# A fused long-convolution and cosine feed-forward kernel: shorter transforms of batches 2 to 7, 29 instead of 31 main chunks, and a last part that begins 940 tokens sooner

## The chip, the core and the metric

The kernel runs on one core of a Trainium2 chip. The engines are PE (the matmuls; its weight loads are shown apart as PEld), DVE (vector), ACT (scalar), POOL (GpSimd) and SP (which issues most of the DMAs). Each engine works through its own instructions in a fixed order and waits on semaphores where it needs another engine's result. The metric is the device time of one execution in microseconds, lower is better; the number given is the median of several executions.

## What is computed

```python
def _attn_ref(x, filt_r, filt_i):            # x: 8 batches, 3008 tokens, 256 columns
    X = np.fft.rfft(x, axis=1)
    F = (filt_r + 1j * filt_i)[None, :, :]
    return np.fft.irfft(X * F, n=x.shape[1], axis=1)
...
def _moe_ref(x, w_in, w_out):                # the 24064 tokens as rows
    h = x @ w_in                             # 256 -> 2048
    g = h * np.cos(h)
    return g @ w_out                         # 2048 -> 256
```

All is float32. The kernel gets that accuracy from matmuls in a rounded format by splitting a value in a high and a low part and adding three products (high by high, low by high, high by low).

## The kernel before

**Transform.** 3008 is 47 times 64, so each batch's FFT is done in stages with small matrices on PE, and between the stages the data goes through DRAM. Of batches 1 to 7: `stage1` (32 pieces a batch: ACT and POOL split the loaded input, POOL at L358; PE multiplies at L363; DVE copies at L365; SP writes), then `stage23` (12 pieces a batch). A piece of `stage23` is loaded, POOL adds two halves (`zf`, L389), ACT rounds (`zh`, L393), POOL takes the low part (`zl`, L394), PE multiplies by the matrix `m2` (three matmuls, L286, L287, L288; the third needs `zl`) into one of two PSUM banks named `ps`, DVE multiplies by the filter (L404 four times, L405, L406; after L406 the bank is free), ACT and POOL split again (`yh` L409, `yl` L410), PE multiplies by `m3` (the same three lines, into the next `ps` bank), and ACT copies out (L419). `stage4` (units of 235 tokens: PE L555, ACT and DVE L576 to L590, POOL `y1` L591) makes the feed-forward part's input.

**Feed-forward, main part.** Tokens are taken in chunks (`SIZES`), each in 8 steps. A step is `hidden` (12 matmuls at L699, as wide as the chunk, into `hp`), the gate (ACT L709, DVE L710, ACT L713, DVE L714, ACT `gh` L719, POOL `gl` L720) and, two steps later, `project` (12 matmuls at L734). So a chunk takes 192 matmuls of its width.

**Feed-forward, last part.** The tokens from the end of the main chunks on are computed by a scheme of block products with 7 products in place of 8. A chunk there is four quads; a quad is 42 matmuls at L780, half as wide as the chunk (248 or 250 columns), and 24 at L864 of the chunk's width. The function `_wide` cuts the tokens into nearly equal chunks of at most 504. This part cannot begin before batch 7 is transformed, because its first operations combine tokens of different places (the flag is that all of batch 7's `z2` are written); eight DMAs (`load_sums`) bring prepared weight sums.

**What sets the order.** From the third chunk on PE's order is written out by hand: the program walks through the steps of the feed-forward part, and at each quarter step asks a list `due` which transform pieces are due. Time in that list is counted in slots: 64 slots are 470 tokens of a chunk, so a chunk of 510 has 69.4 slots. A piece that PE takes part in keeps at least 3 slots from the one before, except that a batch's `m3` of one piece and `m2` of a later one may stand together. Each batch is spread evenly between a start and an end:

```python
        start = FIRST if b == 1 else end + BETWEEN
        end = slot(NJ * TJ) - BEFORE + LATER if b == 1 else start + LENGTH
...
        step = (end - start - GAP12) / (ones + 2 * n23)
...
            t = start + step * (i - SOON + 1 if b == 1 else 2 * i + 1)
            plan(stage1(b, i), t - AHEAD1, [t, t + step][: b], split=t - SPLIT1 if b > 1 else None)
...
            t = start + step * (ones + 2 * i + 2) + GAP12
            g = stage23(b, i)
            plan(g, t - AHEAD2, [], lambda b=b: len(wrote1.get(b, ())) == 2 * n1, t - SPLIT2)
            due.extend([at, kind, g, lambda: True] for at, kind in ((t, SECOND), (t + 4 * step, THIRD)))
```

So `GAP12` is the pause between the two stages, in which the first stage's results reach DRAM and come back. The second stage's first instructions are emitted behind the gate that was emitted last: `zf` on POOL is tied behind that gate's `gl`, the cast on ACT behind that gate's cast. The order on ACT, DVE, POOL and SP is otherwise a scheduler's.

Of the kernel before, what the change touches and what calls it, by code (L numbers as in the profile page):

```python
# [29 lines left out]
SLOTS = 8  # L30
LAG = 2
APART = 3
FIRST, LENGTH, BETWEEN = 80, 260, 24
BEFORE, LATER = 140, 28
GAP12 = 28
AHEAD1, AHEAD2, AHEAD4 = 34, 36, 24
SPLIT1, SPLIT2 = 18, 20
HALF, WIDE = 252, 512
SIZES = [470] * 4 + [464] + [510] * 26
FROM4, APART4, LATE4, CLOSE4 = 12, 20, 2, 14  # L40
SUMS, EACH_SUM, KEEP = 64, 12, 9
LOAD_SUMS, EACH_LOAD = 2030, 8
AHEAD_UNIT, APART_TIED = 130, 4
AHEAD_BLOCK = (52, 48, 43, 38, 33, 28)
SOON = 4
# [132 lines left out]
def fft_filter_then_cos_glu(ctx: ExitStack, tc: tile.TileContext, ins, outT):  # L178
# [41 lines left out]
    def load_full(*names):  # L220
        for name in names:
            rows, cols = ins[name].shape
            shared = {"f1": "m1", "f1x": "m1", "f2": "m2", "f3": "m3", "f30": "m30"}.get(name)
            mats[name] = const.tile([P, 2 * cols if shared and rows == P else cols], F32, name=name, tag=shared or name)[:rows, :cols]
            nc.sync.dma_start(mats[name], ins[name])
# [8 lines left out]
    begins = [0]  # L234
    for size in SIZES:
        begins.append(begins[-1] + size)
# [293 lines left out]
    def stage4(u):  # L530
# [40 lines left out]
        else:  # L571
            parts = [(k, max(t0, begins[k]), min(t0 + size, begins[k + 1])) for k in range(len(SIZES)) if max(t0, begins[k]) < min(t0 + size, begins[k + 1])]
            flat = fft.tile([P, 512], F32, name="y4", bufs=1)[:, : NDT * size].rearrange("p (t n) -> p t n", t=NDT)
# [115 lines left out]
    def hidden(c, s):  # L689
        nt = SIZES[c]  # L690
        yh, yl = ys[c]
        assert filled[c] == nt, (c, filled)
        hp = ps_h.tile([P, 2, 512], F32, name="hp")
        for u in range(2):
            fs = slice(u * P, (u + 1) * P)
            for t in range(NDT):
                for n, (w, y) in enumerate(((0, yh), (0, yl), (1, yh))):
                    with tc.issue_after(last_h[0]) if c == s == 0 else nullcontext():
                        mm = nc.tensor.matmul(hp[:, u, :nt], w_in[s][w][:, t, fs], y[:, t, :nt],  # L699
                                              start=(t == 0 and n == 0), stop=(t == NDT - 1 and n == 2))  # L700
                if u == 0 or t == 0:
                    yield
        last_h[:] = [mm.ins]
        with tc.high_priority() if c == 0 else nullcontext():
            gs[c, s] = gate(hp[:, :, :nt], nt, nc.vector if c == 0 else nc.gpsimd)
# [18 lines left out]
    def project(c, s):  # L724
        nt = SIZES[c]
        if s == 0:
            accs[c] = [ps_o.tile([P, 512], F32, name=f"acc{e}") for e in range(2)]
        gh, gl = gs.pop((c, s))
        for e in range(2):
            acc = accs[c][e][:, :nt]  # L730
            es = slice(e * P, (e + 1) * P)
            for u in range(2):
                for n, (w, g) in enumerate(((0, gh), (1, gh), (0, gl))):
                    nc.tensor.matmul(acc, w_out[s][w][:, u, es], g[:, u],  # L734
                                     start=(s == 0 and u == 0 and n == 0),
                                     stop=(s == NFT // 2 - 1 and u == 1 and n == 2))
                if e == 0 or u == 0:
                    yield
        if s == NFT // 2 - 1:
            t0 = begins[c]  # L740
            for e in range(2):
                if stages:
                    o = fft.tile([P, 512], F32, name="o", tag="ld", bufs=5)[:, :nt]
                else:
                    o = opool.tile([P, 510], F32, name="o")[:, :nt]
                nc.scalar.activation(o, accs[c][e][:, :nt], AF.Copy, scale=TWO_PI)
                nc.scalar.dma_start(outT[e * P : (e + 1) * P, t0 : t0 + nt], o)
            del accs[c], ys[c]
# [234 lines left out]
    with tc.issue_after(last_x[0]):  # L983
        load_full("m40", "m41")
    steps = [(c, s) for c in range(len(SIZES)) for s in range(NS)]

# [33 lines left out]
    for b in range(1, B):  # L1020
        start = FIRST if b == 1 else end + BETWEEN
        end = slot(NJ * TJ) - BEFORE + LATER if b == 1 else start + LENGTH
        ones = n1 - SOON if b == 1 else 2 * n1
        step = (end - start - GAP12) / (ones + 2 * n23)
        for i in range(SOON if b == 1 else 0, n1):
            t = start + step * (i - SOON + 1 if b == 1 else 2 * i + 1)
            plan(stage1(b, i), t - AHEAD1, [t, t + step][: b], split=t - SPLIT1 if b > 1 else None)
        for i in range(n23):
# [4 lines that stand above are left out]
    for u in range(2, len(units)):  # L1033
# [10 lines left out]
        else:  # L1044
            k = max(k for k in range(len(SIZES)) if begins[k] <= t0)
            place = sum(begins[k] <= a < t0 for _, _, a in units)
# [157 lines left out]
```

## Time and profile before

| | |
|---|---|
| time, median of 3 executions | 2404.26 us (2403.96 to 2405.15) |
| the profiled execution's own time | 2405.0 us |
| its span | 2403.2 us |
| TensorE clock over the span, as a share | 0.997 |

Busy time is what an engine spends in instructions, and a bracket behind an instruction of a listing in order of time is the idle time just before it with what ended it. A listing gives the start in us, the busy time of the group, the engine, the line, the operation, the tiles and the shapes; the ends of matmuls are modelled, so prices of matmuls are taken from start to start.

### The profile page before, as it was taken

How to read it: one execution, taken by the hardware profiler on the slowest of the kernel's cores; microseconds unless marked ns; L12 is line 12 of the kernel's file. 1: busy time of each engine (PE TensorE's matmuls, PEld its weight loads, DVE VectorE, ACT ScalarE, POOL GpSimd, SP SyncE). 2: the span in 40 equal slices, each digit the busy share in tenths (PEclk: the TensorE clock that was granted, in tenths of full speed). 3: DMA queues.
4: the chain of work that ended last, by engine and by line, in shares of the span. 5: the costliest groups of instructions: out<-in, count | busy, mean ns of one | idle time of the engine just before them, and what ended most of it. 6: DMA issues, size and time to landing. Idle time of an engine off the chain costs nothing.

```text
span 2403.2 us, 35048 instructions
## 1 busy us (share of the span) xinstructions
PE 2367.4 (99%) x12127; PEld 1999.8 (83%) x12127; DVE 1641.4 (68%) x2328; ACT 1658.2 (69%) x2469; POOL 1820.3 (76%) x1465
## 2 busy tenths in 40 slices
PE   6999999999999999999999999999999999999999
PEld 2788888888888888878887888888999999999998
DVE  5846756766686677658666765855777777777776
ACT  4866676767677666767676776766767777676776
POOL 2777677978797787869787887956777777777775
PEclk9999999999999999999999999999999999999999
DMA  8745355545554554545445444540000000000000
GB/s 296 250 145 157 121 150 148 177 141 141 156 186 129 144 186 142 145 139 183 133 139 183 153 135 127 186 127 27 25 18 30 22 27 25 22 26 26 23 13 18
DMA packets 187433, 277.53 MB, mean 115 GB/s; under 512 B 19344, under 2 KB 102480, under 8 KB 187256
## 3 DMA queue, kind: packets, MB, share of 16 engines
q1 hardware_dynamic: 155448, 223.11, 31.0%
q10 hardware_dynamic: 31808, 52.18, 6.0%
q8 instruction: 97, 1.59, 0.3%
q14 instruction: 80, 0.66, 0.1%
HBM read 177.16 MB, written 98.06 MB: 115 GB/s over the span
## 4 chain that ended last, share of the span: by engine, by line
PE 89%; POOL 2%; DVE 2%; issue 1%; ACT 1%; DMA 0%; SPq 0%; ACTq 0%; POOLq 0%; DVEq 0%
PE acc L734 25%; PE hp L699 25%; PE acc L864 15%; PE x L780 8%; PE w L780 4%; PE ps L555 3%; PE ps L780 2%; PE ps L363 2%; PE ps L288 2%; PE ps L286 1%; PE ps L287 1%; POOL gl L720 1%; POOL zl L394 0%; POOL zf L389 0%; DVE g L710 0%
## 5 line engine op out<-in xcount | busy, mean ns | idle before, releaser
L720 POOL TENSOR_TENSOR gl<-g,gh 128x1020 fp32r<-128x1020 f32 (+2 forms) x240 | 570.8, 2378 | 236.5 <-ACT gh L719 129.4
L699 PE MATMUL hp<-y,w_in 128*128 128x510 f32 (+2 forms) x2976 | 737.7, 390 | 4.3 <-DVE g L714 3.6
L699 PEld LDWEIGHTS hp<-y,w_in 128*128 128x128 f32 x2976 | 560.7, 189 | 124.1 <-issue 5.3
L734 PE MATMUL acc<-gh,w_out 128*128 128x510 f32 (+2 forms) x1984 | 613.4, 391 | 0.0
L710 DVE TENSOR_TENSOR g<-g,hp 128x1020 f32<-128x1020 int32 (+2 forms) x248 | 297.9, 1201 | 203.8 <-ACT g L709 202.3
L734 PEld LDWEIGHTS acc<-gh,w_out 128*128 128x128 f32 x1984 | 367.9, 188 | 75.3 <-issue 2.0
L714 DVE TENSOR_TENSOR g<-g,hp 128x1020 f32<-128x1020 f32 (+2 forms) x248 | 297.7, 1201 | 133.0 <-ACT g L713 131.4
L734 PE MATMUL acc<-gl,w_out 128*128 128x510 f32 (+2 forms) x992 | 384.4, 389 | 0.7 <-POOL gl L720 0.5
L713 ACT ACTIVATE g<-g,half_pi 128x1020 f32<-128x1020 f32 (+2 forms) x248 | 282.5, 1139 | 147.6 <-DVE g L710 143.8
L719 ACT CAST gh<-g 128x1020 fp32r<-128x1020 f32 (+2 forms) x248 | 256.9, 1036 | 136.5 <-DVE g L714 135.5
L709 ACT ACTIVATE g<-hp 128x1020 int32<-128x1020 f32 (+2 forms) x248 | 250.2, 1009 | 141.4 <-PE hp L699 118.5
L358 POOL TENSOR_TENSOR xh<-xf,xh 48x512 fp32r<-48x512 f32 x192 | 244.4, 1292 | 0.0
L762 ACT ACTIVATE qg<-qg,half_pi 128x496 f32<-128x496 f32 (+1 forms) x272 | 187.4, 711 | 70.4 <-DVE qg L761 70.2
L734 PEld LDWEIGHTS acc<-gl,w_out 128*128 128x128 f32 x992 | 186.7, 188 | 41.3 <-POOL gl L720 2.1
L365 DVE COPY z1t<-ps 96x512 f32<-96x512 f32 x192 | 131.6, 685 | 114.1 <-PE ps L363 110.9
L404 DVE SCALAR_TENSOR_TENSOR sw<-ps,sg,f 64x256 f32<-64x256 f32 x336 | 162.4, 483 | 56.7 <-PE ps L288 51.7
L864 PE MATMUL acc<-hg,w_out 128*128 128x496 f32 (+1 forms) x548 | 183.8, 390 | 0.0
L864 PE MATMUL acc<-hgh,w_out 128*128 128x496 f32 (+1 forms) x544 | 182.9, 390 | 0.6 <-POOL hgh L842 0.6
L864 PE MATMUL acc<-hgl,w_out 128*128 128x496 f32 (+1 forms) x540 | 181.3, 390 | 0.0
L410 POOL TENSOR_TENSOR yl<-ya,yh 128x512 fp32r<-128x512 f32 x84 | 109.2, 1301 | 37.5 <-ACT yh L409 29.0
L786 ACT COPY sum<-x 128x496 f32<-128x496 f32 (+1 forms) x136 | 78.4, 577 | 63.7 <-PE x L780 63.4
L394 POOL TENSOR_TENSOR zl<-zf,zh 128x512 fp32r<-128x512 f32 x84 | 108.9, 1299 | 9.9 <-ACT zh L393 9.8
(162 smaller groups left out, 4176.9 us busy)
## 6 DMA issues: line engine op xcount, KB each, us to landing
xf<-in_x SPq DMA_DIRECT2D x224, 192.0 KB
z<-z1t SPq DMA_DIRECT2D x192, 192.0 KB
z<-z SPq DMA_DIRECT2D x98, 240.0 KB
f<-in_fb SPq DMA_DIRECT2D x84, 256.0 KB
f<-in_fa SPq DMA_DIRECT2D x84, 256.0 KB
zf<-z SPq DMA_DIRECT2D x84, 256.0 KB
z<-z2t ACTq DMA_DIRECT2D x84, 256.0 KB
zg<-z SPq DMA_DIRECT2D x72, 256.0 KB
```

The lines of the kernel that those rows point to most:

```text
L358: nc.gpsimd.tensor_tensor(xh[:Q], xf[:Q, v], xh[:Q].bitcast(F32), ALU.subtract)
L699: mm = nc.tensor.matmul(hp[:, u, :nt], w_in[s][w][:, t, fs], y[:, t, :nt], start=(t == 0 and n == 0), stop=(t == NDT - 1 and n == 2))
L709: rounded = nc.scalar.activation(g.bitcast(I32), h, AF.Copy, bias=0.25)
L710: rest = nc.vector.tensor_tensor(g, g.bitcast(I32), h, ALU.subtract)
L713: sine = nc.scalar.activation(g, g, AF.Sin, bias=half_pi, scale=-TWO_PI)
L714: mult = nc.vector.tensor_tensor(g, g, h, ALU.mult)
L719: cast = nc.scalar.copy(gh, g)
L720: lower = engine.tensor_tensor(gl, g, gh.bitcast(F32), ALU.subtract)
L734: nc.tensor.matmul(acc, w_out[s][w][:, u, es], g[:, u], start=(s == 0 and u == 0 and n == 0), stop=(s == NFT // 2 - 1 and u == 1 and n == 2))
L762: nc.scalar.activation(g, g, AF.Sin, bias=half_pi, scale=-TWO_PI)
L780: nc.tensor.matmul(bank[:, p * n : (p + 1) * n], ws[a], y[b], start=first and p == i == 0, stop=last and i == 2, skip_group_check=True)
L864: nc.tensor.matmul(acc, w[a][:, u, e * P : (e + 1) * P], b[:, :, p], start=(q, u, p, n) == (0, 1, 0, 0), stop=(end and p == 1 and n == 2))
```

## The change

The main part shrinks from 31 chunks (15604 tokens) to 29 (14664): a chunk of 470, the one of 464 and one of 510 go, and one of 504 comes. The last part grows from 8460 to 9400 tokens, from 17 chunks (10 of 496 tokens, 7 of 500) to 19 (13 of 496, 6 of 492). A batch's transform has 250 slots in place of 260, 34 of them the pause in place of 28; the pause between batches is 18 in place of 24. In slots, batch 7 ran from 1741.6 to 2001.6 and the last part began at 2124.9; now it runs from 1655.6 to 1905.6, and the last part begins at 1996.8. A step inside a batch is 3.86 slots in place of 4.14.

```diff
-FIRST, LENGTH, BETWEEN = 80, 260, 24
+FIRST, LENGTH, BETWEEN = 80, 250, 18
 BEFORE, LATER = 140, 28
-GAP12 = 28
+GAP12 = 34
...
-SIZES = [470] * 4 + [464] + [510] * 26
+SIZES = [470] * 3 + [504] + [510] * 25
...
-LOAD_SUMS, EACH_LOAD = 2030, 8
+LOAD_SUMS, EACH_LOAD = 1924, 6
```

The order on POOL where the second stage of batch 6 begins, before. `gl` is the gate's low part, `zf` and `zl` are as above, and the number behind a name tells one buffer from another; `zl_11954` is the batch's first.

```order
L720 TENSOR_TENSOR gl_11918<-g_11912,gh_11917 128x2x510
L389 TENSOR_TENSOR zf_11886<-zf_11886,zg_11887 128x512
L720 TENSOR_TENSOR gl_11970<-g_11964,gh_11969 128x2x510
L389 TENSOR_TENSOR zf_11921<-zf_11921,zg_11922 128x512
L394 TENSOR_TENSOR zl_11954<-zf_11886,zh_11953 128x512
L394 TENSOR_TENSOR zl_11997<-zf_11921,zh_11996 128x512
```

The same place after the change; the batch's first low part is now `zl_11595`.

```order
L720 TENSOR_TENSOR gl_11578<-g_11572,gh_11577 128x2x510
L389 TENSOR_TENSOR zf_11491<-zf_11491,zg_11492 128x512
L591 TENSOR_TENSOR y1_11467<-y4_11654,y0_11466 128x2x235
L720 TENSOR_TENSOR gl_11630<-g_11624,gh_11629 128x2x510
L389 TENSOR_TENSOR zf_11540<-zf_11540,zg_11541 128x512
L389 TENSOR_TENSOR zf_11581<-zf_11581,zg_11582 128x512
L394 TENSOR_TENSOR zl_11595<-zf_11491,zh_11594 128x512
L394 TENSOR_TENSOR zl_11638<-zf_11540,zh_11637 128x512
```

Behind the last `gl` one `zf` stood ahead of the first `zl`; now two do.

PE at the same place before, from the last matmul into `hp_11939` (the source of `gl_11970`) to the batch's first L288, with 63 rows between; of each run of equal rows one stands.

```order
L699 MATMUL hp_11939<-y0_11285,w_in1_4_89 128x510
...
L699 MATMUL hp_11985<-y0_11285,w_in0_5_90 128x510
...
L734 MATMUL acc0_11876<-gh_11917,w_out0_3_102 128x510
...
L699 MATMUL hp_12031<-y0_11285,w_in0_6_92 128x510
...
L555 MATMUL ps_12065<-m40_617,z4_11928 128x120
...
L734 MATMUL acc0_11876<-gh_11969,w_out0_4_104 128x510
...
L286 MATMUL ps_12088<-zh_11953,m2_1479 128x512
L287 MATMUL ps_12088<-zh_11953,m2_1479 128x512
L288 MATMUL ps_12088<-zl_11954,m2_1479 128x512
```

PE at that place after the change, from the last matmul into `hp_11607` (the source of `gl_11630`) to the batch's first L288, with 39 rows between.

```order
L699 MATMUL hp_11607<-y0_11016,w_in1_3_87 128x510
...
L555 MATMUL ps_11649<-m40_617,z4_11501 128x120
...
L734 MATMUL acc1_11586<-gh_11521,w_out0_1_98 128x510
...
L699 MATMUL hp_11667<-y0_11016,w_in0_4_88 128x510
...
L734 MATMUL acc0_11585<-gh_11577,w_out0_2_100 128x510
...
L286 MATMUL ps_11710<-zh_11594,m2_1485 128x512
L287 MATMUL ps_11710<-zh_11594,m2_1485 128x512
L288 MATMUL ps_11710<-zl_11595,m2_1485 128x512
```

One `hidden` (12 rows) and one `project` (12 rows) that stood between the gate's source and the batch's first L288 are no longer there.

PE inside the second stage of batch 6 before, where one piece's `m3` and a later piece's `m2` stand together; `ps_12375` takes the bank that `ps_12309` had.

```order
L288 MATMUL ps_12309<-zl_12119,m2_1479 128x512
...
L699 MATMUL hp_12334<-y0_11751,w_in0_2_84 128x510
...
L286 MATMUL ps_12368<-yh_12232,m3_1482 128x512
L287 MATMUL ps_12368<-yh_12232,m3_1482 128x512
L288 MATMUL ps_12368<-yl_12233,m3_1482 128x512
L286 MATMUL ps_12375<-zh_12177,m2_1479 128x512
```

PE inside the second stage of batch 3 after the change, at such a place; `ps_6433` takes the bank that `ps_6389` had.

```order
L288 MATMUL ps_6389<-zl_6203,m2_1485 128x512
...
L699 MATMUL hp_6416<-y0_5464,w_in0_7_94 128x510
...
L286 MATMUL ps_6426<-yh_6312,m3_1488 128x512
L287 MATMUL ps_6426<-yh_6312,m3_1488 128x512
L288 MATMUL ps_6426<-yl_6313,m3_1488 128x512
L286 MATMUL ps_6433<-zh_6268,m2_1485 128x512
```

Between the L288 and the L286 of the same bank stood 18 rows, at three places; now there are 15 at three places (one in batch 3, two in batch 7) and 18 at one.

## Rows read from the trace of the kernel before

**Rows 1.** The page: busy engines, granted clock by slices, and chain that ended last.

```profile
PE 2367.4 (99%) x12127; PEld 1999.8 (83%) x12127; DVE 1641.4 (68%) x2328; ACT 1658.2 (69%) x2469; POOL 1820.3 (76%) x1465
...
PEclk9999999999999999999999999999999999999999
...
PE 89%; POOL 2%; DVE 2%; issue 1%; ACT 1%; DMA 0%; SPq 0%; ACTq 0%; POOLq 0%; DVEq 0%
```

**Rows 2.** The timeline of PE: hidden steps of chunks of 470, 464 and 510.

```profile
223.93 2.72 PE L699 MATMUL hp<-y,w_in 128*128 128x470 f32 x12
226.49 0.59 PE L734 MATMUL acc<-gh,w_out 128*128 128x470 f32 x2
...
283.28 2.67 PE L699 MATMUL hp<-y,w_in 128*128 128x464 f32 x12
285.78 0.58 PE L734 MATMUL acc<-gh,w_out 128*128 128x464 f32 x2
...
1646.40 2.88 PE L699 MATMUL hp<-y,w_in 128*128 128x510 f32 x12
1649.12 0.61 PE L734 MATMUL acc<-gh,w_out 128*128 128x510 f32 x2
```

**Rows 3.** The timeline of PE: quads of the last part, by their first products.

```profile
2024.76 0.85 PE L780 MATMUL x<-y,w_in 128*128 128x248 f32 x6
...
2035.85 0.84 PE L780 MATMUL x<-y,w_in 128*128 128x248 f32 x6
...
2067.50 0.86 PE L780 MATMUL x<-y,w_in 128*128 128x250 f32 x6
...
2075.10 1.05 PE L555 MATMUL ps<-m,z 120*128 120x120 f32 x8
2075.92 0.70 PE L864 MATMUL acc<-hg,w_out 128*128 128x500 f32 x2
...
2078.76 0.87 PE L780 MATMUL x<-y,w_in 128*128 128x250 f32 x6
```

**Rows 4.** The timeline of PE where batch 5's second stage begins.

```profile
1075.20 0.50 PE L288 MATMUL ps<-zl,m 128*128 128x512 f32 x1 [2.30 <-POOL zl L394]
1075.54 4.49 PE L699 MATMUL hp<-y,w_in 128*128 128x510 f32 x12
1079.83 1.08 PE L555 MATMUL ps<-m,z 120*128 120x120 f32 x8
```

**Rows 5.** The timeline of ACT and POOL at that place.

```profile
1064.36 1.03 ACT L709 ACTIVATE g<-hp 128x1020 int32<-128x1020 f32 x1 [1.73 <-PE hp L699]
...
1070.29 2.41 POOL L720 TENSOR_TENSOR gl<-g,gh 128x1020 fp32r<-128x1020 f32 x1 [0.18 <-POOL zf L389]
...
1072.66 1.26 POOL L389 TENSOR_TENSOR zf<-zf,zg 128x512 f32<-128x512 f32 x1
1073.88 2.52 POOL L394 TENSOR_TENSOR zl<-zf,zh 128x512 fp32r<-128x512 f32 x2
```

**Rows 6.** Windows: us, busy PE, PEld, DVE, ACT, POOL, clock, DMA share, GB/s.

```profile
1077.00:1080.00 3.00, 3.00 (x10) 2.35 (x9) 2.09 (x4) 0.00 (x0) 2.98 (x2) 0.52 0.49 156
1502.00:1594.00 92.00, 90.51 (x413) 74.20 (x412) 72.83 (x106) 63.48 (x86) 77.43 (x53) 1.00 0.59 187
```

**Rows 7.** All waits of PE for `zl`: us in total, times, longest.

```profile
PE ps L288 <- POOL zl L394: 4.7, 3, 2.3
```

**Rows 8.** The timeline of PE at a pair of pieces in batch 6.

```profile
1311.69 0.39 PE L288 MATMUL ps<-zl,m 128*128 128x512 f32 x1
...
1316.96 0.50 PE L286 MATMUL ps<-zh,m 128*128 128x512 f32 x1 [0.76 <-DVE ya L406]
```

**Rows 9.** Groups by line and shape of DVE: count, busy us, mean ns, idle before.

```profile
L404 DVE SCALAR_TENSOR_TENSOR sw<-ps,sg,f 64x256 f32<-64x256 f32 x336 | 162.4, 483 | 56.7 <-PE ps L288 51.7
...
L405 DVE TENSOR_TENSOR ps<-ps,f 128x512 f32<-128x512 f32 x84 | 58.5, 696 | 1.6
L406 DVE TENSOR_TENSOR ya<-ps,sw 128x512 f32<-128x512 f32 x84 | 57.9, 689 | 5.2
```

## The prediction

> **What bounds the kernel now.** I read the page first. PE is busy 99% of the span, the chain that ended last is 89% PE, the others have 1 or 2% each, and the granted clock is full in all 40 slices [rows 1]. POOL is next with 76%, DVE and ACT have under 70%. So a term of the forecast is one of two things: PE's own work priced start to start, or a wait of PE. Next I read the timeline of PE for clean prices by width. A `hidden` of twelve matmuls takes 226.49 − 223.93 = 2.56 us at 470 columns, 285.78 − 283.28 = 2.50 at 464, 1649.12 − 1646.40 = 2.72 at 510 [rows 2]. A quad of the last part at 248 columns takes 2035.85 − 2024.76 = 11.09, and eight L555 matmuls in it belong to `stage4`; these take 2075.92 − 2075.10 = 0.82, so the quad takes 10.27. At 250 it is 2078.76 − 2067.50 − 0.82 = 10.44 [rows 3]. Last came the list of waits: POOL's `zl` held PE's L288 three times, 4.7 us together, 2.3 the longest [rows 7]. That one is where batch 5's second stage begins [rows 4, 5].
>
> **A. The columns.** A main chunk is 16 groups of twelve (8 `hidden`, 8 `project`). Out go a chunk of 470 (16 × 2.56 = 41.0), one of 464 (16 × 2.50 = 40.0) and one of 510 (16 × 2.72 = 43.5); in comes one of 504, which between the 470 and the 510 comes to 43.1. Main part: −81.4. A chunk of the last part is four quads: 41.1 at 496 tokens, 41.8 at 500. For 492 no row exists. On the line through the two it is 40.4; if the narrow L780 matmul gets no cheaper below 248 and only the 96 L864 lose four columns each (96 × 4 columns at the 2.72 / 12 / 510 us that a column costs, 0.17), it is 40.9. Before: 10 × 41.1 + 7 × 41.8 = 703.6. After: 13 × 41.1 + 6 × 40.4 = 776.7, or with 40.9, 779.7. Last part: +73.1 to +76.1. So A lies between −8.3 and −5.3. I take −6.4, nearer the dear end, since of the 0.17 between a quad at 248 and at 250 the columns alone (42 × 2 + 24 × 4 = 180 at that price, 0.08) explain half. The transforms' own matmuls are the same in number and size.
>
> The row for 510 columns is 2.72 / 12 = 227 ns a matmul, and at 250 to 248 columns a quad still loses 0.17 us [rows 2, 3]. The Trainium skill, page "TensorE: Matmul & The Clock Gate", sections "Back-to-back issue gap" and "LDWEIGHTS (loading the stationary operand)", would have 215 ns for 510 (columns at 2.4 GHz plus 2.5 ns), and 107 ns for a load of 128 weight columns, which is more than 246 to 250 columns take, so that all L780 cost the same. By it I estimate 38.1 + 37.6 + 41.3 − 40.8 = 76.2 us less in the main part, 74.1 more in the last one, and A = −2.1; the sum below would come to +4.4. The rows disagree with it in size and in the step from 250 to 248, and I go by the rows.
>
> **B. Where the second stage begins.** `zf` and `zl` are queued on POOL behind the latest `gl`. In batch 5 that gate began at 1064.36 (its `hp` just finished); its `gl` ended at 1072.7, 8.3 us later; one `zf` (1.26) and one `zl` (1.26) brought it to 1075.1, 10.8 us after [rows 5]. PE had 38 rows in between in the order, some 8.7 us, and so waited 2.30 [rows 4]. Behind the wait the granted clock was 0.52 [rows 6], near the lower of its two levels (1.2 of 2.4 GHz), and twelve L699 took 1079.83 − 1075.54 = 4.29 instead of 2.72: 1.6 more [rows 4]. What stands behind the waiting L288 is the whole of PE, so the wait is on the path in full. Batch 5 has the same order after the change: 0 (from −1.6, if the clock holds this time). In batch 6 63 rows (14.4 us) stood in between, more than 10.8, and there was no wait. Now there are 39: 33 of 510 columns at 0.227, four L555 at 0.2 (two records each, half of 0.82 / 4), two at 0.23, together 8.8 us. POOL now has two `zf` ahead of the first `zl`: 8.3 + 3 × 1.28 = 12.2. PE waits 12.2 − 8.8 = **+3.4**, and a fall of the clock as in batch 5 adds **+1.6**. Bounds: 0, if the gate's chain runs ahead, and 6.6, if the clock stays down twice as long. The other two waits for `zl` are 4.7 − 2.3 = 2.4 together [rows 7]; one of them (batch 4's second piece) shrinks by 0.4 in the new order, the other (batch 7's tenth) loses the `gl` ahead of it, −1.2, and single rows fewer in batches 2 and 3 give +0.6. B = 5.0 − 1.0 = **+4.0**.
>
> **C. Two banks.** Pieces that stand together need a bank back from the piece before. After its L288 DVE works 4 × 0.483 + 0.696 + 0.689 = 3.3 us [rows 9], behind whatever gate operation DVE has. In batch 6 the bank came free 1316.96 − 1311.69 = 5.3 us after L288 began, of which PE waited 0.76 [rows 8]. With 18 rows between, PE arrives after 19 × 0.227 = 4.3 to 4.5; with 15, after 3.6. Before, three such places with 18 rows cost 1.2 in all. Now three have 15 (each 0.3 more than 0 if the bank takes 3.9, 1.7 if it takes 5.3; I take 0.8) and one has 18 (0.3). C = 2.7 − 1.2 = **+1.5**, between 0 and +3.
>
> **D. One late unit.** The last `y1` (L591) before the seventh chunk stands on POOL behind a `gl` (2.41 [rows 5]) and two more low parts (2 × 1.28), and its L555 now is only 7.1 us of PE ahead of the chunk that reads it. PE to ACT to POOL and back takes some 8: **+1.0**, between 0 and +3.
>
> **E. What costs nothing.** The pause of 34 slots gives the last first-stage piece 25.8 to 28.1 us to the first `m2`, by PE's order at the prices above, in place of 22.2 to 24.4; nothing in before's list of waits is PE waiting for these loads, so more room brings nothing. It only pays for the steps between pieces: 12 pieces of `stage23` in 82.5 us of PE, in place of 87 to 90. POOL's work there is 36 × 1.29 plus some 12 `gl` of 2.41, 75.6 us, 92% of it, in place of 77.4 in a window of 92 [rows 6]: it fits. Batch 7's end to the last part's start shrinks from 107 slots to 75, some 48 us; the first L555 of the last part stand 47 us ahead of it in place of 65 and stay covered. The earlier eight loads go with the room that the batch's end has.
>
> **Sum.** −6.4 + 4.0 + 1.5 + 1.0 = +0.1: 2405.1 for the profiled execution of 2405.0 (span 2403.2 plus 1.8 around it), which stood 0.7 above the median. On the median that is 2404.4; I say **2404.2**. 0.2%, 4.8 us, is about what a measurement of this kernel can tell from no change.
>
> **Rivals.**
> 1. *The seam in batch 6 doesn't stall, or PE makes it up.* For it: no such wait is in the trace of before at that batch, and a schedule on the chip may let `gl` end sooner. Against: POOL's order is fixed, and batch 5 shows its price. Without B's 5.0 the sum is −4.9: 2399.4, and with C and D at 0, 2397. Chance 0.22.
> 2. *POOL becomes the bound in the shorter second stages.* At 92% of 82.5 us it has 6.9 us of slack per batch; a `gl` that is late by more than that holds the `project` behind it. The place is the middle of a second stage. Each event costs a wait like batch 5's (2.3 [rows 4]) and the fall of the clock (1.6), 3.9. From two events beyond B on it decides: +0.1 + 7.8 gives 2412; with one, 2408, still within 0.2%. Against it: in the window of 92 us PE waited little though POOL had 84%. Chance 0.17.
> 3. *The wider pause removes the waits where second stages begin.* If they hung on the loads, batch 5's 3.9 and the new one would both go: −6.4 − 3.9 − 2.4 = 2391.6. Against: the releaser is POOL's `zl` [rows 4, 7], whose place follows from the order. Chance 0.04.
> 4. *The last part begins before its input is there.* 48 us in place of 68 for step 4 and the loads of the sums. A DMA that comes 10 us late adds these 10: 2414. No wait of that kind is in before. Chance 0.04.
>
> The forecast itself has 0.53. Its own range, from the bounds of A to D, is 2399.6 to 2409. Rival 1 is nearly all below the limit of 2399.5 (0.20 of 0.22), and so is rival 3; of rival 2 0.12 lie above 2409.1, with rival 4 0.16. The forecast's own tails give 0.02 on either side. So faster 0.26, same 0.56, slower 0.18, and the range that leaves out 2 in 10 is 2396.5 to 2411.
>
> **What the new profile would show.** Right: a wait of PE L288 for `zl` of about 3.4 us where batch 6's second stage begins, beside the 2.3 of batch 5; clock near 0.5 for some 3 us behind both; two or three waits of L286 for `ya` L406 of about a us; quads of 10.1 to 10.25 us at 246 columns. Wrong: no wait in batch 6 (rival 1), several waits for `gl`, `zl` or `yl` in the middle of second stages (rival 2), no wait in batch 5 (rival 3), an idle PE or waits for DMAs around the first L780 (rival 4). What would upset it most is the granted clock: whether it falls behind a wait is worth 1.6 us each time, and this trace shows it at one place only.

## The result, and the profile after

The changed kernel takes 2421.02 us (median of 6 executions, 2420.01 to 2421.68) against 2403.96 (median of 5) for the kernel before beside it: the ratio is 1.007, with an interval of 1.006 to 1.0081. It is slower by 17 us, beyond the range that was given. One execution of the kernel before (2768.89 us) and one of e6 (2916.29 us) ran far slower than all others and are left out of the medians. The profiled execution took 2421.67 us with a span of 2420.0.

The page of the changed kernel, with the lines that answer to [rows 1]:

```profile
PE 2373.7 (98%) x12271; PEld 2004.8 (83%) x12271; DVE 1675.6 (69%) x2396; ACT 1666.3 (69%) x2518; POOL 1841.1 (76%) x1515
...
PEclk8999999999999999999999999999999999999999
...
PE 91%; DVE 3%; DMA 2%; POOL 1%; ACT 1%; issue 1%; SPq 0%; DVEq 0%; ACTq 0%; POOLq 0%
```

At this height little shows, except that a DMA has 2% of the chain where it had 0. The list of PE's waits (us in total, times, longest) tells more:

```profile
PE ps L288 <- POOL zl L394: 8.1, 4, 4.1
PE ps L555 <- DMA z<-z: 6.5, 1, 6.5
...
PE ps L286 <- DVE y L578: 1.4, 4, 0.5
PE ps L286 <- ACT z2t L419: 1.4, 2, 0.7
PE acc L734 <- POOL gl L720: 1.0, 1, 1.0
PE ps L288 <- POOL yl L410: 0.8, 1, 0.8
```

The first line answers to [rows 7]: 4.7 became 8.1, where the forecast's terms give 4.7 + 3.4 − 1.0 = 7.1. The second is new, and no term of the sum had it.

For a complete account I took, for each matmul of the two traces, the time to the next one's start less the median for its line and shape. These excesses sum to 44.3 us before and 63.1 after, and what is left (the medians alone) is 2351.1 and 2348.9. So of 16.8 us of span, +18.8 are waits and a low clock and −2.2 are medians, that is, columns. The columns' share is known to about a us only: the medians of L699, L734, L780 and L864 alone give −3.0, and the same account of e5 and e6 below, which have the same columns as these two kernels, gives −1.2. The excesses by what they stand in front of, where one is over 0.15 us, before and after: L555 0.2 and 6.9, L288 5.5 and 10.0, L286 3.3 and 5.3, matmuls of the main part at the low clock 1.4 and 3.3; the start of the last part in all 2.6 and 4.2. What lies ahead of the third chunk is alike, 26.3 and 26.2. The shorter ones behind it come to 3.0 and 5.3.

**The new wait.** The timeline of PE, then that of ACT, then that of SP of the changed kernel, where batch 1 ends, ahead of the sixth chunk:

```profile
312.93 0.40 PE L288 MATMUL ps<-yl,m 128*128 128x512 f32 x1
...
321.93 2.03 PE L555 MATMUL ps<-m,z 120*128 120x120 f32 x8 [6.52 <-DMA z<-z]
323.63 4.10 PE L699 MATMUL hp<-y,w_in 128*128 128x510 f32 x9
327.56 0.40 PE L363 MATMUL ps<-xh,m 96*96 96x512 f32 x1
...
313.88 1.15 ACT L357 CAST xh<-xf 96x512 fp32r<-96x512 f32 x2
314.93 0.58 ACT L419 COPY z2t<-ps 128x512 f32<-128x512 f32 x1
...
315.54 0.33 ACTq L421 DMA_DIRECT2D z<-z2t  x1
...
317.62 1.30 SPq L543 DMA_DIRECT2D z<-z  x3
```

The L288 at 312.93 is the last matmul of batch 1's last piece. ACT copies its result at 314.93, behind two casts of batch 2, writes it to DRAM at 315.54, SP, which had waited 5.2 us for this write, loads it at 317.62, and L555 has its data at 321.93: 9.0 us after the L288. In PE's order only nine rows stand between that L288 and the L555, 2.3 us with the L288 itself, and so PE waits 6.52. The same two places in the timeline of PE before:

```profile
313.23 0.39 PE L288 MATMUL ps<-yl,m 128*128 128x512 f32 x1
...
322.54 1.05 PE L555 MATMUL ps<-m,z 120*128 120x120 f32 x8
```

There they are 9.3 us apart, with 41 rows between them, and PE did not wait. What moved is a chunk boundary. The unit holds the tokens 2914 to 3148, of which those from 3008 on need batch 1. Before, a chunk ended at 2854, and the unit belonged to the next one alone. Now the sixth chunk ends at 2934, so twenty of its tokens come from this unit, and the unit's L555 is due before the sixth chunk begins (at 331.48). Behind the wait the matmuls run at half speed: the eight L555 take 323.63 − 321.93 = 1.70 instead of 0.82 [rows 3], nine L699 take 3.93 instead of 2.04 (9 × 0.227). With these 2.8 the place costs 9.3 us.

**Where the second stage of batch 6 begins.** PE, then POOL:

```profile
1255.70 0.62 PE L288 MATMUL ps<-zl,m 128*128 128x512 f32 x1 [4.15 <-POOL zl L394]
...
1257.39 3.81 PE L699 MATMUL hp<-y,w_in 128*128 128x510 f32 x12
1261.04 0.62 PE L734 MATMUL acc<-gh,w_out 128*128 128x510 f32 x2
...
1249.55 2.42 POOL L720 TENSOR_TENSOR gl<-g,gh 128x1020 fp32r<-128x1020 f32 x1
1251.90 2.52 POOL L389 TENSOR_TENSOR zf<-zf,zg 128x512 f32<-128x512 f32 x2
1254.35 2.53 POOL L394 TENSOR_TENSOR zl<-zf,zh 128x512 fp32r<-128x512 f32 x2
```

`gl`, two `zf`, then `zl`, as the order said, and PE waits 4.15 against a forecast of 3.4. The clock fell here too. In batch 5, where the wait is 2.32 again, it did not. These windows (us, busy PE, PEld, DVE, ACT, POOL, clock, DMA share, GB/s) are the three us behind each wait:

```profile
1255.50:1258.50 3.00, 2.80 (x7) 2.23 (x8) 2.06 (x5) 0.01 (x1) 3.00 (x3) 0.57 0.68 197
1048.50:1051.50 3.00, 3.00 (x13) 2.50 (x14) 2.40 (x5) 0.60 (x1) 3.00 (x2) 1.00 0.71 201
```

**The columns.** A step of the chunk of 504, and a quad of 492 tokens, in the timeline of PE:

```profile
226.42 2.90 PE L699 MATMUL hp<-y,w_in 128*128 128x504 f32 x12
229.16 0.61 PE L734 MATMUL acc<-gh,w_out 128*128 128x504 f32 x2
...
1979.25 0.85 PE L780 MATMUL x<-y,w_in 128*128 128x246 f32 x6
1979.93 1.05 PE L555 MATMUL ps<-m,z 120*128 120x120 f32 x8
...
1990.39 0.85 PE L780 MATMUL x<-y,w_in 128*128 128x246 f32 x6
```

Twelve matmuls of 504 take 2.74 here, and 2.72 to 2.74 in the chunk's other steps: no less than the 2.72 of 510 [rows 2]. The quad of 492 takes 1990.39 − 1979.25 − 0.82 = 10.32, more than the 10.27 of 496 [rows 3]. (Quads without L555 take 10.26 at 492, 10.21 at 496 and 10.39 at 500, so eight L555 among a quad's rows cost 0.89 and not the 0.82 that was taken off; it shifts all of these alike.) Put in the forecast's own sum, the main part gives 41.0 + 40.0 + 43.5 − 16 × 2.74 = 80.7 less, the last part 13 × 41.1 + 24 × 10.32 − 703.6 = 78.4 more: −2.3 in place of −6.4.

### The profile page after: what moved, and what is told of

Its sections match the earlier page's. It is cut to its first block, busy times and chain, and to the rows that moved or that the text cites. A ratio compares the mean times of both kernels' runs of the same rounds, so it can differ in the third digit from the quotient of the medians.

```text
span 2420.0 us, 35532 instructions
## 1 busy us (share of the span) xinstructions
PE 2373.7 (98%) x12271; PEld 2004.8 (83%) x12271; DVE 1675.6 (69%) x2396; ACT 1666.3 (69%) x2518; POOL 1841.1 (76%) x1515
## 4 chain that ended last, share of the span: by engine, by line
PE 91%; DVE 3%; DMA 2%; POOL 1%; ACT 1%; issue 1%; SPq 0%; DVEq 0%; ACTq 0%; POOLq 0%
PE hp L699 24%; PE acc L734 24%; PE acc L864 17%; PE x L780 9%; PE w L780 4%; PE ps L555 4%; PE ps L780 2%; PE ps L363 2%; PE ps L286 1%; PE ps L288 1%; PE ps L287 1%; DVE g L710 1%; DVE sw L404 1%; DMA ff<-in_fa 1%; DVE g L714 1%
## 5 line engine op out<-in xcount | busy, mean ns | idle before, releaser
L720 POOL TENSOR_TENSOR gl<-g,gh 128x1020 fp32r<-128x1020 f32 (+2 forms) x224 | 535.3, 2390 | 236.8 <-ACT gh L719 128.2
L699 PE MATMUL hp<-y,w_in 128*128 128x510 f32 (+2 forms) x2784 | 695.2, 391 | 4.3 <-DVE g L714 3.6
L699 PEld LDWEIGHTS hp<-y,w_in 128*128 128x128 f32 x2784 | 526.4, 189 | 119.7 <-issue 5.5
L734 PE MATMUL acc<-gh,w_out 128*128 128x510 f32 (+2 forms) x1856 | 576.3, 393 | 0.0
L734 PEld LDWEIGHTS acc<-gh,w_out 128*128 128x128 f32 x1856 | 344.8, 188 | 72.6 <-issue 2.5
L734 PE MATMUL acc<-gl,w_out 128*128 128x510 f32 (+2 forms) x928 | 360.6, 391 | 1.0 <-POOL gl L720 1.0
L762 ACT ACTIVATE qg<-qg,half_pi 128x496 f32<-128x496 f32 (+1 forms) x304 | 208.6, 709 | 84.8 <-DVE qg L761 84.8
L734 PEld LDWEIGHTS acc<-gl,w_out 128*128 128x128 f32 x928 | 174.8, 188 | 39.0 <-POOL gl L720 1.5
L864 PE MATMUL acc<-hg,w_out 128*128 128x496 f32 (+1 forms) x612 | 204.9, 389 | 0.6 <-POOL hg L842 0.6
L864 PE MATMUL acc<-hgl,w_out 128*128 128x496 f32 (+1 forms) x608 | 203.4, 389 | 0.0
L864 PE MATMUL acc<-hgh,w_out 128*128 128x496 f32 (+1 forms) x604 | 202.5, 389 | 0.0
L780 PE MATMUL x<-diff,sum 128*128 128x248 f32 (+1 forms) x912 | 129.2, 277 | 0.6 <-ACT sum L786 0.6
```

The costliest lines, as they stand in the source:

```text
L720: lower = engine.tensor_tensor(gl, g, gh.bitcast(F32), ALU.subtract)
L734: nc.tensor.matmul(acc, w_out[s][w][:, u, es], g[:, u], start=(s == 0 and u == 0 and n == 0), stop=(s == NFT // 2 - 1 and u == 1 and n == 2))
L762: nc.scalar.activation(g, g, AF.Sin, bias=half_pi, scale=-TWO_PI)
L780: nc.tensor.matmul(bank[:, p * n : (p + 1) * n], ws[a], y[b], start=first and p == i == 0, stop=last and i == 2, skip_group_check=True)
L864: nc.tensor.matmul(acc, w[a][:, u, e * P : (e + 1) * P], b[:, :, p], start=(q, u, p, n) == (0, 1, 0, 0), stop=(end and p == 1 and n == 2))
```

## The experiments

Two theories of the new wait: the place of the chunk boundary (theory 1), or the denser transforms, whose batch 2 begins sooner and gets in the way (theory 2). For the waits for `zl` and the banks: the place at which a batch's pieces meet the gates, or a POOL that is full in a shorter second stage.

**e1, the transforms alone** (in the kernel before).

```diff
-FIRST, LENGTH, BETWEEN = 80, 260, 24
+FIRST, LENGTH, BETWEEN = 80, 250, 18
-GAP12 = 28
+GAP12 = 34
```

> The kernel before with the new transforms alone (250 slots, pauses of 34 and 18); chunks and last part as before. Theory 1, the chunk boundary: the 6.5 us wait of L555 for its load at 315 us of the changed kernel comes from the new chunk sizes, so here there is none; by the order, batch 5's and batch 6's first L288 have room again, and two waits of 0.6 us are left of some 5 us of waits and 1.5 us of low clock before: about 2400 us. Theory 2, the denser transforms: batch 2 begins 6 slots sooner, its casts and loads stand ahead of batch 1's last copy and hold the unit up; then the wait of 6 us and the low clock behind it (2 us and more) are here too: 2408 us or more.

Measured: 2409.79 us against 2403.83, ratio 1.0026 (1.0016 to 1.0036). There is no wait of L555 at the end of batch 1, so on that theory 1 holds, though batch 2 begins as early as in the changed kernel. But the time is not the 2400 expected. PE's waits in this trace:

```profile
PE ps L288 <- POOL zl L394: 2.7, 2, 2.1
PE ps L286 <- ACT z2t L419: 2.0, 3, 0.7
PE ps L286 <- DVE y L578: 1.9, 5, 0.6
PE ps L288 <- POOL yl L410: 1.0, 2, 0.7
```

The wait in batch 5 is gone, as expected; one of 2.1 in batch 7 that I hadn't seen in the order came up, and PE's waits for a bank (L286) are 4.8 in all where the trace before has 2.3; by the account above, with the short ones, 7.3 where before has 3.3. So some 4 of the 6 us that the new transforms cost by themselves stand in front of L286. This is what term C is about: pieces 3.86 slots apart meet the two banks more often too soon.

**e2, batch 1 ends sooner** (in the changed kernel).

```diff
-        start = FIRST if b == 1 else end + BETWEEN
-        end = slot(NJ * TJ) - BEFORE + LATER if b == 1 else start + LENGTH
+        start = FIRST if b == 1 else end + BETWEEN + (14 if b == 2 else 0)
+        end = slot(NJ * TJ) - BEFORE + LATER - 14 if b == 1 else start + LENGTH
```

> The changed kernel, but batch 1's transform ends 14 slots (some 9 us) sooner; all later batches where they were. Theory 1: batch 1's last piece now has 11 us of PE to the unit's L555 in place of 2.3, against a need of 9, so the wait of 6.7 us and the low clock behind it (some 2.8 us) go: 2411.5 us. Theory 2: batch 2 begins where it did, so its casts and loads still stand in the way; at most half of it goes: 2416 us or more.

Measured: 2413.81, ratio 1.0041 (1.0029 to 1.0054): 7.2 us below the changed kernel (8.7 between the profiled spans), nearer theory 1's 2411.5 than theory 2's 2416, though short of theory 1's 9.5. Batch 1's last L288 and the unit's L555 in the timeline of PE:

```profile
303.78 0.40 PE L288 MATMUL ps<-yl,m 128*128 128x512 f32 x1
...
312.91 1.05 PE L555 MATMUL ps<-m,z 120*128 120x120 f32 x8
```

They are 9.1 us apart, and PE does not wait there.

**e3, units cut at the end of batch 0** (in the changed kernel).

```diff
-    pairs = [5] * 8 + [3] * 4 + [5] * ((2 * B * NJ - 52) // 5)
+    pairs = [5] * 8 + [3] * 4 + [4] * 3 + [3] + [5] * 89
```

> The changed kernel with the units of step 4 cut at the end of batch 0 (three units of 188 tokens and one of 141 after token 2444, one unit more in all), so that no unit of the chunk that ends at token 2934 needs batch 1. Theory 1: the wait of 6.7 us and the low clock go, one more unit costs 0.8: 2412 us. Theory 2: nothing about batch 2 changes, so the wait stays with whichever unit comes first after batch 1: 2420 us.

The three units of four pairs meet a matrix laid out for odd counts, so their 564 tokens come out wrong; the work and its order are as intended. Measured: 2414.57, ratio 1.0048 (1.0035 to 1.006). The time is 2.6 above the expected 2412; in this trace the clock also fell behind batch 5's wait, which is worth some 1.6 and which the changed kernel's trace does not have. The wait of L555 is gone with batches 1 and 2 where they were in the changed kernel. So theory 2 falls: the wait came from the unit that straddles both the chunk's end and the batch's end. The two casts of batch 2 that stood ahead of the copy are a part of the 9 us, 1.1 us of it.

**e4, batch 6 three slots later** (in the changed kernel).

```diff
-        start = FIRST if b == 1 else end + BETWEEN
+        start = FIRST if b == 1 else end + BETWEEN + {6: 3, 7: -3}.get(b, 0)
```

> The changed kernel with batch 6 three slots later and batch 7 where it was: by the order, batch 6's first L288 then has PE work enough ahead of it. Theory of the queue on POOL: the wait of 4.1 us and the low clock behind it (1.6) go, all else stays: 2415.3 us. Rival, POOL is full in the shorter second stages: the wait moves to other pieces of batch 6 and the time stays near 2420.

Measured: 2419.66, ratio 1.007 (1.0057 to 1.0084). The wait of 4.15 is gone, but some 20 us later in the same batch there is another, which I had not seen since I had looked at the last gate ahead of each `zl` only. PE, then POOL:

```profile
1274.14 0.50 PE L288 MATMUL ps<-zl,m 128*128 128x512 f32 x1 [2.20 <-POOL zl L394]
...
1267.96 2.42 POOL L720 TENSOR_TENSOR gl<-g,gh 128x1020 fp32r<-128x1020 f32 x1
1270.33 2.53 POOL L389 TENSOR_TENSOR zf<-zf,zg 128x512 f32<-128x512 f32 x2
1272.81 1.28 POOL L394 TENSOR_TENSOR zl<-zf,zh 128x512 fp32r<-128x512 f32 x1
```

Both theories are still open after this. So I worked the waits out from the orders of PE, POOL, ACT and DVE together, each instruction with the duration that the traces show, ready when its inputs and its bank are. That gives 2.4 in batch 5 and 4.3 in batch 6 of the changed kernel (measured 2.32 and 4.15) and 2.9 in batch 7 of e1 (2.1). With it I looked for a place of each batch at which little waits.

**e5 and e6, all batches moved by a few slots**, in the changed kernel (with batch 1 as in e2) and in the kernel before; lengths, pauses inside a batch, chunks and tail of each unchanged.

The first pair of lines stands in e5, the second in e6:

```diff
-        start = FIRST if b == 1 else end + BETWEEN
+        start = FIRST if b == 1 else end + BETWEEN + {2: 10, 3: 4, 4: 2, 5: 1, 6: 2, 7: 1}.get(b, 0)
...
-        start = FIRST if b == 1 else end + BETWEEN
+        start = FIRST if b == 1 else end + BETWEEN + {2: -1, 3: 3, 5: -4, 6: 1, 7: 3}.get(b, 0)
```

> The changed kernel with batch 1 ending 14 slots sooner and batches 2 to 7 moved by -4, 0, 2, 3, 5 and 6 slots, so that by the orders of PE, POOL, ACT and DVE no second stage begins behind a late gate; lengths, pauses inside a batch, chunks and last part as in the changed kernel. Theory of the queue and the place: the waits inside the transforms (11 us and 1.6 of low clock) and the unit's wait (9.5 with its low clock) shrink to some 2 us: 2398 us, between 2395 and 2401. Rival, the shorter second stages fill POOL whatever the place: waits come up elsewhere and it stays above 2408. If the columns are worth the forecast -6.4, it is below the next kernel by 4 us or more; if they are worth -2.5, the two are equal within 3.

> The kernel before with batches 2 to 7 moved by -1, 2, 2, -2, -1 and 2 slots for the same reason; all else as before. Theory of the queue and the place: before's waits in the transforms (some 8.8 us and 1.5 of low clock) go: 2395 us, between 2393 and 2398. Rival: before's waits are of the stages' density and stay: 2403.

Measured: e5 2400.89, ratio 0.9984 (0.9975 to 0.9993), 13 us below e2; e6 2398.49, ratio 0.9976 (0.9967 to 0.9986), half a us above the range expected. PE's waits in e5:

```profile
PE ps L286 <- ACT z2t L419: 1.4, 2, 0.7
PE ps L286 <- DVE y L578: 1.3, 5, 0.4
...
PE ps L288 <- POOL zl L394: 0.3, 1, 0.3
```

The waits for `zl` fell from 8.1 to 0.3 in second stages as short as the changed kernel's, so POOL is not full in them: the place decides. e5 is not below e6 by 4 us but 2.4 above it. Between the two spans (2399.1 and 2396.0) lie, by the same account as above, −1.2 of medians, +1.5 in front of L286, +0.8 in front of L288, +1.5 at the start of the last part, and +0.5 of others; so the columns are not worth 6.4. The intervals of the two ratios overlap; the order of e5 and e6 is not settled by them.

**e7, the inner pause back at 28** (in the changed kernel).

```diff
-GAP12 = 34
+GAP12 = 28
```

> The changed kernel with the inner pause back at 28 slots, so that the pieces have 3.96 slots each in place of 3.86 and all of them change place. Theory of the place: by the orders, waits of 2 to 4 us arise where batches 2, 4, 5 and 6 are in their second stage and before two chunks, 6 to 8 us more than in the changed kernel: 2427 us. Rival, density: pieces that stand further apart wait less: 2415 to 2419.

Measured: 2430.04, ratio 1.0107 (1.0093 to 1.012). Pieces further apart, and slower by 9 us: the rival, density, falls, and the theory of the place came within 3 us. Its waits:

```profile
PE ps L288 <- POOL zl L394: 10.9, 4, 3.8
PE ps L555 <- DMA z<-z: 4.8, 1, 4.8
...
PE hp L699 <- POOL y L591: 2.6, 1, 2.6
```

**e8, other widths in the last part** (on top of e5).

```diff
-    sizes = [(tokens // 4 * (k + 1) // count - tokens // 4 * k // count) * 2 for k in range(count)]
+    sizes = [244 if k in (6, 12, 18) else 248 for k in range(count)]
```

> The first of these kernels (batches moved), with the last part's 9400 tokens cut in 16 chunks of 496 and 3 of 488 in place of 13 of 496 and 6 of 492. The trace of the changed kernel has quads of 492 tokens at 10.26 us and of 496 at 10.21. Theory of odd widths (492 and 500 cost extra against widths that eight divides): a quad of 488 takes 10.05 to 10.10, the whole 1.2 to 1.9 us less than the first kernel. Rival, the weight loads bind the narrow products: 10.15 to 10.2 at 488 and a difference under 0.8 us.

Measured: 2396.41, ratio 0.997 (0.9959 to 0.9982), 4.5 us below e5. A quad of 488 tokens without L555:

```profile
1860.74 0.84 PE L780 MATMUL x<-y,w_in 128*128 128x244 f32 x6
1870.80 0.85 PE L780 MATMUL x<-y,w_in 128*128 128x248 f32 x6
```

10.06, as the theory of widths said (10.05 to 10.10). The gain of the whole is larger than the 1.2 to 1.9 expected: the medians of the two traces differ by 3.6. The expectation's own prices already give more than it said: 24 quads at 10.26 and 52 at 10.21 against 12 at 10.06 and 64 at 10.21 is 3.0.

**e9, the same thought in the kernel before** (on top of e6).

```diff
-    sizes = [(tokens // 4 * (k + 1) // count - tokens // 4 * k // count) * 2 for k in range(count)]
+    sizes = [252 if k in (3, 8, 13) else 250 if k == 16 else 248 for k in range(count)]
```

> The kernel before with its batches moved as in the run that did only that, and its last part's 8460 tokens cut in 13 chunks of 496, 3 of 504 and 1 of 500 in place of 10 of 496 and 7 of 500. Quads of 500 took 10.39 us there and of 496 10.21. If widths that eight divides are the cheap ones, a quad of 504 takes 10.30 to 10.40 (eight columns more than 496, at the 0.02 us a column between 488 and 496), and the whole is 1 to 2 us less than that run: 2397 us. If the price only follows the columns from 492 on, a quad of 504 takes 10.5 and the whole is the same within 0.5 us: 2398.6.

Measured: 2396.29, ratio 0.9964 (0.995 to 0.9977), 2.2 below e6. A quad of 504 takes 10.36, no more than one of 500 (10.38). Beside e8 (0.30%) this is the fastest version, 0.36% below the kernel before.

**e10, a table of widths** in the main part of the kernel before, one profiled execution.

```diff
-SIZES = [470] * 4 + [464] + [510] * 26
+SIZES = [470] * 4 + [464] + list(range(510, 470, -2)) + [492] * 6 + [488]
```

> The kernel before with its 26 chunks of 510 replaced by 27 of all even widths from 510 to 472, six of 492 and one of 488, to read the start-to-start price of a matmul at each width in one trace. If eight (or sixteen) decides, the price per column is lowest at 472, 480, 488, 496 and 504, and at 492 and 500 some 2 to 4 ns a matmul lie above the line through these. If the main part knows no such rule, as its 227 ns at 510 against 225 at 496 of the last part hints, the price rises evenly with the width. The time itself says little: one chunk more and other places of the transforms; some 2410 to 2440 us.

Measured: 2425.75. Two widths in the timeline of PE:

```profile
1503.98 2.80 PE L699 MATMUL hp<-y,w_in 128*128 128x492 f32 x12
1506.62 0.60 PE L734 MATMUL acc<-gh,w_out 128*128 128x492 f32 x2
...
637.20 2.88 PE L699 MATMUL hp<-y,w_in 128*128 128x498 f32 x12
639.92 0.61 PE L734 MATMUL acc<-gh,w_out 128*128 128x498 f32 x2
```

2.64 for twelve of 492, and 2.72 for twelve of 498, as much as for 510 [rows 2]. The price does not rise evenly, and eight does not decide either: both readings that I had offered are wrong in the main part. What it does is told at the end.

## Why the prediction was wrong, point by point

**What bounds the kernel** was right: PE's own work or a wait of PE, and all of the 17 us is one or the other. Of the 16.7 us of span between the forecast's +0.1 and the measured +16.8, D is 8.3, A 4.2 and the start of the last part 1.6; the rest is spread over small places. The range was also narrower than the bounds of its own terms, which add up to 2395 to 2410.6; 2421 lies outside these too.

**The step that failed is D, "one late unit".** It found the right unit and put down +1.0, at most +3, for POOL's `y1` behind a `gl`. The place cost 9.3: 6.5 of waiting for the load and 2.8 of low clock (e2 and e3 take the wait away). I had looked at who waits for the unit, 7.1 us of PE ahead of the chunk, and not at what the unit waits for. Its L555 stands nine rows of PE behind batch 1's last matmul, and the result of that matmul reaches it by ACT's copy, a write to DRAM and a load, 9.0 us in all. (The chunk is the sixth; the prediction calls it the seventh, whose unit began 8.5 us ahead of it in the trace after, 373.15 to 381.61, and held nothing up.) Rival 4, a DMA that comes late, named this mechanism at the wrong place, the start of the last part, and with 0.04. Its argument, that no wait of that kind is in the trace before, was no help: a new order makes new neighbours.

**A, the columns, was mis-sized:** −6.4 forecast, within −8.3 to −5.3; measured −2.2 by medians and −2.3 by the forecast's own sum (−1.2 to −3.0 by the other ways of counting above), outside the bounds. Both bounds rested on one thought, that fewer columns cost less. 504 columns cost as much as 510, and a quad of 492 tokens costs more than one of 496.
The Trainium skill, page "TensorE: Matmul & The Clock Gate", sections "Back-to-back issue gap" and "LDWEIGHTS (loading the stationary operand)", had led to an estimate of −2.1, near what was measured, but not by the prices: L780 took 115 ns at 246 and 248 columns and 113 at 244, where the page's weight load would make it 107 for all, and 510 columns took 227 ns, not the 215 of its formula for an isolated matmul. The trace agrees only in that 246 brought nothing over 248.

**B, where second stages begin, was right** in place, cause and nearly in size: batch 6 waits 4.15 (forecast 3.4) with 1.6 of low clock, batch 5 waits 2.32 again. That batch 5's clock held this time (−1.6) was in the bounds. Moving the batches (e5, e6) takes these waits away and shows the cause.

**C, two banks,** was right in its mechanism and its bounds: +1.5 forecast, and in front of L286 the account has +2.0. The three places with 15 rows (693.32, 1486.95 and 1526.45 us) cost 0.8, 0.8 and 0.3, the one with 18 cost 0.2, together 0.8 more than the three of before; the other 1.2 of the +2.0 stand before L286 that C had not counted. At two of the places the profile puts the wait down to ACT's L419 instead of DVE's L406, but L406 ended within 0.02 us of each L286 there (693.30 and 1486.94).

**E:** the pause as such costs nothing that e7 shows, but changing it moves every piece, which is worth 9 us there. The start of the last part came out 1.6 dearer, which I had at nothing. Every run with the new chunks shows there a wait of 1.0 of L734 for `gl`, and no run with the old ones does (0.5 at most, in two waits); what in the new chunks makes it was not tried.

**Rival 2**, a full POOL, falls with e5 and e7. **Rival 1** fell with the wait in batch 6. Its thought, that without B the change would gain, is not borne out either: with nearly all waits gone e5 is 2.4 us above e6, two numbers whose intervals overlap.

## What to carry to other kernels

When a chunk boundary moves, look at each piece that lies across it from both sides: how far ahead of its reader it stands, and how far behind its last producer, with the whole way through DRAM (9 us here) in between. Waits on an engine with a fixed order can be worked out from the orders of all engines and the durations of one trace, to between 0.1 and 0.8 us in the three places compared here; a few slots for each batch were worth more (5.9 us in the kernel before) than all columns of this change (some 2). And price a matmul's width from a trace of that very width.

## What the runs showed of the hardware

**Widths.** The table of e10, start to start over twelve matmuls of L699: 213 ns at 470, 472 and 478 columns (215 at 476), 217 at 480, 220 at 482, 486, 490 and 492, 223 at 494 and 496, 227 at 498, 500, 506 and 510 (225 at 502, one group; 228 at 504). The price does not rise evenly: it is flat from 482 to 492 and nearly flat from 498 to 510, so 492 is cheap and 498 dear. In the last part, where narrow and wide matmuls alternate, the medians are 220 ns at 488, 226 at 492, 225 at 496, 229 at 500: there 492 is dear. No run here shows why.

**The clock.** The same wait of 2.3 us in batch 5 was followed by a granted clock near half (1.2 of 2.4 GHz) in two traces, that of before [rows 6] and that of e3, and by the full clock in three, those of the changed kernel, e2 and e4. The window behind the wait in e3:

```profile
1039.00:1042.00 3.00, 3.00 (x7) 2.37 (x8) 2.21 (x5) 0.50 (x1) 3.00 (x2) 0.50 0.67 199
```

It also fell behind waits of 1.8 us (e7), 2.1 (e1) and 2.2 (e4). Behind the waits of 4.15 and 6.5 us it fell in each trace that has them. So a wait of 2.3 us is worth 2.3 or 3.9, and the runs do not show what decides it.

**The way through DRAM.** In the changed kernel, from the write's issue to the load's is 2.1 us (315.54 to 317.62), from there to L555 4.3. The Trainium skill, page "DMA: Bandwidth & Descriptors", section "Anatomy of one DMA — SWDGE (gpsimd) path", has some 2 us of fixed cost and the bytes at 436 GB/s, which for the two transfers of 256 and 240 KB I estimate at 5.2 us; the 6.4 here, on other queues than the page's, is somewhat more.
